# Summing four query-key chunks of the last block by accumulating DMAs instead of pair adds on GpSimd

## The chip, the cores and the metric

One core of one Trainium2 chip runs the whole kernel. The metric is the device time of one execution in microseconds (us). A single core has no die to compare with, so a run is called fast when it lies within 1.5% of the fastest run of the same kernel. Ratios are the mean time of one kernel's fast runs over the mean of the other's fast runs of the same rounds, so they are not quite the ratio of the medians quoted beside them.

Engines: PE is TensorE's matmuls, PEld its weight loads, DVE is VectorE, ACT is ScalarE, POOL is GpSimd, SP is SyncE, which issues most DMAs. "L816" is line 816 of the kernel. The change adds 25 lines in the middle, so lines below it move: L816 becomes L841, L1052 becomes L1077, and so on.

## The reference, cut to what matters

```python
xn = _layernorm(x)                                   # 2048 positions x 640
# A: local attention, 32 heads of 20, window of 8 keys at distance 0, 2, ..., 14
logits = einsum("bhsd,bhswd->bhsw", q, kg) * scale   # kg: keys gathered at the 8 offsets
attn   = softmax(where(mask, logits, -1e9))
o      = einsum("bhsw,bhswd->bhsd", attn, vg)
# B: gated branch
h      = (xn @ w_gate) * (xn @ w_up)                 # 640 -> 1536
return x + o.reshape(...) @ wo + h @ w_down
```

The 2048 positions are handled as four blocks `j` of 512. The 640 columns of q and k are five chunks `c` of 128 partitions. With 20 columns per head, a head is spread so that each chunk holds four elements of every head.

## The kernel before: the parts that matter

A query-key logit is made in two steps. VectorE multiplies q by a shifted k, elementwise. TensorE then sums the products over partitions and chunks with a 0/1 matrix `G`. For most blocks that is five chunks, so five accumulating terms per head sum. In the last block (`WIDE`) the first four chunks take q straight from PSUM, give FP32 products in half-size pieces (`PRD32`), and GpSimd adds two chunks at a time. Three terms remain: chunks 0+1, chunks 2+3, and chunk 4. There are two key halves `r`, so six terms, and four matmuls for each.

```python
def pair_add(j, s, n, q0, f, parts):                 # last block only
    a, b = PRD32[f[0]], PRD32[f[1]]
    o = s[:, q0:q0 + 2, :]
    def go():
        op("pool", lambda e: e.tensor_tensor(o, a[:], b[:], ALU.add), ..., occ=2.36, lock=True)
        free.extend(f)
        parts.append(q0)
    yield Task("pool", go, ..., prio=5, lock=True)

def logits(j, slots):                                # the head sums on TensorE (L816)
    ...
    yield Task("pe", go, r=[e[1][:] for e in slots], prio=9.5, banks=2, slack=0.5)
    bump("lg")
```

The program of each engine is fixed while the kernel is built. A list scheduler in the kernel's own code takes tasks in order of an assumed time. For that it uses a duration per operation (`occ`) and, for a DMA, a byte count (`nbytes`) and an added delay (`extra`). On the chip a late input holds up everything behind it in the list: in the traces here TensorE stands still for up to 13.77 us at one such input.

Three gates hang on the last head-sum block:

```python
def vx_loads():                  # values for the weighted sums; they reuse q's memory
    yield num(NJ, "lg")          # all four head-sum blocks have been placed
    ...
def weighted():                  # PV = attention weight x value on VectorE (L962),
    ...                          # pair adds on GpSimd (L967), select-sums on TensorE (L1008)
def gu(j):                       # gate and up projections, 12 pairs per block, PE filler
    ...
    if j == 1 and m == 6:
        yield num(NJ, "lg")      # pair 19 and later reuse a product buffer
```

The weighted stage has 20 units (block x chunk). A select-sum takes three units at a time. The down projection `dn(j)` needs all units of its block and is also what lets the gate/up pairs of the fourth block start.

## Time and profile before

| | before |
|---|---|
| two runs | 271.29 and 348.41 us (median 309.85) |
| profiled run | 271.47 us, span 269.7 us |
| 23 further runs, on three later occasions | 271.06 to 272.17 us |

The first and fourth parts of the page: busy time, share of the span and instruction count by engine, then the chain of work that ended last.

```profile
PE 264.3 (98%) x1791; PEld 152.7 (57%) x1791; DVE 231.9 (86%) x294; ACT 98.4 (36%) x175; POOL 115.2 (43%) x65
...
PE 96%; DVE 2%; DMA 1%; issue 0%; DVEq 0%
```

TensorE is the limit almost everywhere. The windows of before show the second limit. Columns: the stretch, its length, then busy us and instruction count of PE, PEld, DVE, ACT and POOL, granted TensorE clock, DMA share, GB/s.

```profile
80.00:108.00 28.00, 28.00 (x145) 12.78 (x145) 25.25 (x29) 7.66 (x13) 18.41 (x8) 1.00 0.61 141
108.00:121.00 13.00, 13.00 (x74) 5.75 (x63) 12.79 (x14) 6.78 (x10) 3.27 (x1) 1.00 0.55 146
...
160.00:180.00 20.00, 20.00 (x150) 13.36 (x148) 18.54 (x17) 2.45 (x5) 15.45 (x7) 1.00 0.52 137
```

Third busy number: VectorE is busy 38.0 of the 41 us from 80 to 121 us. It has almost nothing to give away, although TensorE is the engine that never stops.

The timeline of TensorE before, at two places: the last head sums (L816), and the select-sum of units 3 to 5 (L1008) with the first down projection (L1110) after it. Columns: start, duration, engine, line, operation, output<-inputs, shapes, count; brackets would show idle time and who ended it.

```profile
107.20 1.48 PE L816 MATMUL PS<-PRD,G 128*32 128x512 bf16 x24
108.61 1.25 PE L1052 MATMUL PS<-XNT,WG 128*128 128x512 bf16 x5
...
162.10 0.83 PE L1008 MATMUL PS<-SV,SEL 128*32 128x512 bf16 x12
162.87 1.80 PE L1110 MATMUL PS<-WD,HT 128*128 128x320 bf16 x12
```

No wait of PE shows at either place.

### The profile page before, as it was taken

The numbers are of one execution on the slowest core, as the hardware profiler recorded it, in microseconds if no ns is written. First come the engines' busy times: TensorE is split into PE (matmuls) and PEld (weight loads), VectorE is DVE, ScalarE is ACT, GpSimd is POOL, SyncE is SP. The second block draws the span as 40 slices with busy tenths as digits, with TensorE's granted clock in tenths as the row PEclk, the third lists the DMA queues.
The fourth block names the chain that finished last, engine by engine and source line by source line (L and its number), as shares of the span: only waits on it lengthen the run. The fifth ranks groups of instructions, "written<-read, shape, count | busy, mean of one in ns | idle before, by whom it ended". The sixth has DMA issues, their size and how long they took to land.

```text
span 269.7 us, 4474 instructions
## 1 busy us (share of the span) xinstructions
PE 264.3 (98%) x1791; PEld 152.7 (57%) x1791; DVE 231.9 (86%) x294; ACT 98.4 (36%) x175; POOL 115.2 (43%) x65
## 2 busy tenths in 40 slices
PE   7999999999999999999999999999999999999995
PEld 4896965544444444443444446764447767654775
DVE  4778899999999997999999999989999998984221
ACT  2469998557632123632324422015240120033000
POOL 1000000000018763042776676957868679755000
DMA  7966479322325934901295333555333655220101
GB/s 209 366 198 86 99 124 381 158 97 97 104 44 163 216 66 130 282 5 30 52 256 125 86 79 79 155 153 130 79 80 106 175 135 148 66 81 2 49 27 50
DMA packets 39717, 33.49 MB, mean 124 GB/s; under 512 B 15376, under 2 KB 38416, under 8 KB 39696
## 3 DMA queue, kind: packets, MB, share of 16 engines
q1 hardware_dynamic: 39408, 33.15, 45.8%
q8 instruction: 14, 0.23, 0.4%
q10 hardware_dynamic: 288, 0.05, 0.1%
q14 instruction: 7, 0.06, 0.1%
HBM read 25.08 MB, written 5.26 MB: 112 GB/s over the span
## 4 chain that ended last, share of the span: by engine, by line
PE 96%; DVE 2%; DMA 1%; issue 0%; DVEq 0%
PE PS L1052 38%; PE PS L1110 28%; PE PS L610 24%; PE PS L816 3%; PE PS L1008 2%; DMA XST<-in_A_x_dram 1%; PE PS L569 1%; DVE STATS L525 0%; DVE XNT L578 0%; DVE HT L1061 0%; DVE XNS L543 0%; DVE FOUT L1121 0%; DVE MV L528 0%; DVE SD L536 0%; DVEq L319 0%
## 5 line engine op out<-in xcount | busy, mean ns | idle before, releaser
L967 POOL TENSOR_TENSOR SV<-PV 128x1024 bf16<-128x1024 f32 x40 | 94.7, 2378 | 48.4 <-DVE PV L962 48.3
L962 DVE TENSOR_TENSOR PV<-VX,PS 128x1024 f32<-128x1024 bf16 (+1 forms) x56 | 92.7, 1670 | 0.0
L610 PE MATMUL PS<-XNT,WQKV 128*128 128x512 bf16 (+2 forms) x480 | 67.0, 299 | 0.8 <-DVE XNT L578 0.8
L1052 PE MATMUL PS<-XNT,WU 128*128 128x512 bf16 x240 | 59.7, 379 | 0.5 <-DVE HT L1061 0.5
L1052 PE MATMUL PS<-XNT,WG 128*128 128x512 bf16 x240 | 59.7, 379 | 0.0
L610 PEld LDWEIGHTS PS<-XNT,WQKV 128*128 128x128 bf16 x480 | 43.4, 114 | 23.4 <-DVE XNT L578 1.5
L1110 PE MATMUL PS<-WD,HT 128*128 128x320 bf16 (+1 forms) x300 | 43.3, 294 | 0.0
L615 ACT ACTIVATE HT<-PS 128x512 bf16<-128x512 f32 x36 | 21.5, 597 | 53.2 <-PE PS L1052 53.1
L1052 PEld LDWEIGHTS PS<-XNT,WU 128*128 128x128 bf16 x240 | 23.3, 98 | 29.3 <-DVE HT L1061 1.0
L1052 PEld LDWEIGHTS PS<-XNT,WG 128*128 128x128 bf16 x240 | 23.2, 98 | 28.7 <-issue 0.8
L738 DVE TENSOR_TENSOR PRD<-QT,KT 128x2048 bf16<-128x2048 bf16 x32 | 36.8, 1218 | 0.0
L1110 PEld LDWEIGHTS PS<-WD,HT 128*128 128x128 bf16 x300 | 28.5, 98 | 11.6 <-issue 1.3
L794 POOL TENSOR_TENSOR PRD<-PRF,PRF 128x1024 bf16<-128x1024 f32 x8 | 18.8, 2357 | 35.5 <-DVE PRF L780 35.5
L1121 DVE TENSOR_TENSOR FOUT<-PS,XR 128x320 bf16<-128x320 f32 (+1 forms) x33 | 15.8, 478 | 18.3 <-PE PS L1110 18.2
L1061 DVE TENSOR_TENSOR HT<-HT,PS 128x512 bf16<-128x512 bf16 x36 | 24.1, 682 | 6.8 <-PE PS L1052 5.6
L1110 PE MATMUL PS<-WO,OT 128*128 128x320 bf16 (+1 forms) x165 | 27.1, 295 | 0.0
L835 POOL MEMSET LOG<- 32x6 bf16 (+6 forms) x7 | 0.4, 95 | 46.6 <-ACT LOG L827 46.6
L1017 ACT ACTIVATE OT<-PS 128x512 bf16<-128x512 f32 x20 | 10.5, 597 | 25.1 <-PE PS L1008 25.1
L1110 PEld LDWEIGHTS PS<-WO,OT 128*128 128x128 bf16 x165 | 15.9, 98 | 5.9
L780 DVE TENSOR_TENSOR PRF<-PS,KT 128x1024 f32<-128x1024 f32 x16 | 19.0, 1218 | 0.3 <-PE PS L816 0.2
L525 DVE BATCH_NORM_STATS2 STATS<-XST 128x6 f32<-128x320 bf16 x32 | 14.7, 469 | 2.0 <-DMA XST<-in_A_x_dram 2.0
L947 ACT ACTIVATE PS<-ATX 128x512 f32<-128x512 bf16 x8 | 4.8, 598 | 27.4 <-DVE PV L962 27.4
(47 smaller groups left out, 162.3 us busy)
## 6 DMA issues: line engine op xcount, KB each, us to landing
VX<-v_scratch SPq DMA_DIRECT2D x80, 130.0 KB, 2.9
XST<-in_A_x_dram SPq DMA_DIRECT2D x16, 160.0 KB, 6.3
v_scratch<-VST SPq DMA_DIRECT2D x4, 640.0 KB, 4.4
XR<-in_A_x_dram SPq DMA_DIRECT2D x16, 160.0 KB, 3.3
out_dram<-FOUT SPq DMA_DIRECT2D x15, 160.0 KB, 2.0
WG<-in_B_w_gate_dram SPq DMA_DIRECT2D x1, 1920.0 KB, 7.6
WU<-in_B_w_up_dram SPq DMA_DIRECT2D x1, 1920.0 KB, 11.8
WD<-in_B_w_down_dram SPq DMA_DIRECT2D x1, 1920.0 KB, 8.6
```

The costliest lines, as they stand in the source:

```text
L525: op("dve", lambda e: e.bn_stats(o, a), r=[a], w=[("st", t, i)], name=f"bn{t}_{i}", occ=0.49)
L610: op("pe", (lambda o, l, x, c, first: lambda e: e.matmul(o, l, x, start=first, stop=(c == NCH - 1)))(o, l, x, c, first), r=[l, x], w=[o], ...
L615: X = op("act", (lambda o, i: lambda e: e.activation(o, i, ACT.Copy))(o, i), r=[i], w=[o], name=name, occ=0.12 + n * 0.9e-3)
L738: op("dve", lambda e: e.tensor_tensor(s[:], qb, kv, ALU.mult), r=[q, rk], w=[s[:]], name=f"prod{j}_{r}_{c}", occ=1.15, lock=True)
L780: X = op("dve", lambda e: e.tensor_tensor(o[:], qb, kv, ALU.mult), r=[q, rk], w=[o[:]], name=f"prow{j}_{r}_{c}_{q0}", occ=1.17)
L794: op("pool", lambda e: e.tensor_tensor(o, a[:], b[:], ALU.add), r=[a[:], b[:]], w=[o], name=f"padd{j}_{n}_{q0}", occ=2.36, lock=True)
L962: op("dve", lambda e: e.tensor_tensor(p, vw, a, ALU.mult), r=[vv] + rk, w=[p], name=f"pv{u}_{x}_{r0}", occ=0.09 + 1.1 * nr)
L967: X = op("pool", lambda e: e.tensor_tensor(o, p[:, :, 0, :], p[:, :, 1, :], ALU.add), r=[p[:]], w=[o], name=f"pva{u}_{x}", occ=2.36, lock= ...
L1052: op("pe", (lambda l, x, c: lambda e: e.matmul(PS[:, b, :], l, x, start=(c == 0), stop=(c == NCH - 1)))(l, x, c), r=[l, x], w=[PS[:, b, :] ...
L1061: X = op("dve", lambda e: e.tensor_tensor(h, h, PS[:, hold[1], :], ALU.mult), r=[h, PS[:, hold[1], :]], w=[h], name=f"h{m}_{j}", occ=0.65)
L1110: op("pe", (lambda l, x, i: lambda e: e.matmul(dst, l, x, start=(i == 0), stop=(i == n - 1)))(l, x, i), r=[l, x], w=[PS[:, b, :]], name=f" ...
L1121: X = op("dve", lambda e: e.tensor_tensor(o, PS[:, b, 0:wid], xr, ALU.add), r=[PS[:, b, :], xr], w=[o], name=f"fin{t}_{nb}", occ=0.15 + wi ...
```

## The change

The intent: add up all four chunks before TensorE sees them, with DMAs that add what they carry to what lies at the destination (`accum_op`), so that GpSimd does less and only two terms per head sum remain. Eight matmuls fall away. Core of the diff (cut):

```diff
+    def accum(name, a, b):
+        o, i = PRD32[a][:], PRD32[b][:]
+        op("pool", lambda e: e.dma_start(o, i, accum_op=ALU.add), r=[o, i], w=[o], dma=True, name=name, nbytes=1048576,
+           occ=1.0, extra=1.0)
+
+    def gather(name, a, b):                      # chunk pair: a += b; b's buffer is free when it lands
         ...
+    def close(tag, r, q0, acc, f, n, parts):     # chunks 2+3, then onto chunks 0+1
+        yield from gather(f"qacc{tag}_1", *f)
         ...
+        if r:                                    # one more accumulate, and a DMA that casts to BF16
+            yield Task("pool", lambda: accum(f"qacc{tag}_2", acc, f[0]), ...)
+            yield Task("pool", cast, r=[a[:]], w=[o], prio=5)
+        else:                                    # or an add on GpSimd
+            yield Task("pool", add, r=[a[:], b[:]], w=[o], prio=5, lock=True)
-    def pair_add(j, s, n, q0, f, parts):
         ...
-            op("pool", lambda e: e.tensor_tensor(o, a[:], b[:], ALU.add), ..., occ=2.36, lock=True)
```

In all there are ten accumulating DMAs of 512 KB, two casting DMAs of 256 KB and two GpSimd adds, in place of eight GpSimd adds. And because the scheduler assumes long DMAs, the order of everything after them changes. This is TensorE's list from the third head-sum block on (matmul counts; gu = gate/up, 10 per pair; lg = head sums; I = select-sum; dn = down projection):

```
before  lg40 gu35 qkv10 gu80  lg24 gu150 I12 gu90 I12 dn136 I12 gu80 I12 dn136 I12 dn35 I12 dn5 gu40 I8 dn153
changed lg40 gu35 qkv10 gu140 lg16 gu160 I12 gu20 I12 dn119 I12 dn17 gu75 I12 gu5 dn136 I12 dn119 ...
```

More of the change, by code (lines that the diff above doesn't have):

```diff
@@ L755, in wide @@
     def wide(j, slots):
+        sums, parts, dest = {}, {1: [], 0: []}, {}
         for c0 in (0, 2):
@@ L761, in wide @@
                 K.spawn(q_bank(j, c, hold[c]))
-            last = None
             for r in (1, 0):
-                yield lambda: len(free) > 0
-                n = slot()
-                s = PRD[n]
-                parts = []
+                if c0:
+                    yield lambda: len(free) > 0
+                    dest[r] = slot()
                 for q0 in (0, 2):
@@ L785, in wide, with add, cast @@
                         yield Task("dve", go, r=[q, rk], w=[o[:]], prio=20 + j)
-                    K.spawn(pair_add(j, s, n, q0, f, parts))
-                slots.append((n, s, r, parts))
-    def pair_add(j, s, n, q0, f, parts):
-        a, b = PRD32[f[0]], PRD32[f[1]]
-        o = s[:, q0:q0 + 2, :]
-        def go():
-            op("pool", lambda e: e.tensor_tensor(o, a[:], b[:], ALU.add), r=[a[:], b[:]], w=[o], name=f"padd{j}_{n}_{q0}",
-               occ=2.36, lock=True)
-            free.extend(f)
-            parts.append(q0)
-        yield Task("pool", go, r=[a[:], b[:]], w=[o], prio=5, lock=True)
+                    tag = f"{j}_{r}_{q0}"
+                    if c0 == 0:
+                        sums[r, q0] = f[0]
+                        K.spawn(gather(f"qacc{tag}", f[0], f[1]))
+                    else:
+                        K.spawn(close(tag, r, q0, sums[r, q0], f, dest[r], parts[r]))
+        for r in (1, 0):
+            slots.append((dest[r], PRD[dest[r]], r, parts[r]))
+    def accum(name, a, b):
[3 more added lines that the diff above has]
+    def gather(name, a, b):
+        def go():
+            accum(name, a, b)
+            free.append(b)
+        yield Task("pool", go, r=[PRD32[a][:], PRD32[b][:]], w=[PRD32[a][:]], prio=5)
+    def close(tag, r, q0, acc, f, n, parts):
+        yield from gather(f"qacc{tag}_1", *f)
+        o, a, b = PRD[n][:, q0:q0 + 2, :], PRD32[acc], PRD32[f[0]]
+        def add():
+            op("pool", lambda e: e.tensor_tensor(o, a[:], b[:], ALU.add), r=[a[:], b[:]], w=[o], name=f"padd{tag}",
+               occ=2.36, lock=True)
+        def cast():
+            op("pool", lambda e: e.dma_start(o, a[:]), r=[a[:]], w=[o], dma=True, name=f"qcast{tag}", nbytes=786432,
+               occ=1.0, extra=1.0)
+        if r:
+            yield Task("pool", lambda: accum(f"qacc{tag}_2", acc, f[0]), r=[a[:], b[:]], w=[a[:]], prio=5)
+            yield Task("pool", cast, r=[a[:]], w=[o], prio=5)
+        else:
+            yield Task("pool", add, r=[a[:], b[:]], w=[o], prio=5, lock=True)
+        free.extend((acc, f[0]))
+        parts.append(q0)
     def logits(j, slots):
```

## The prediction

> **What bounds the kernel now.** TensorE. The page has PE busy 264.3 of 269.7 us (98%), and the chain that ended last is 96% PE. VectorE is nearly a second limit (231.9 us): the windows leave it only about 8 us of idle between 121 and 247 us. GpSimd (43%) mostly waits for VectorE.
>
> **Removed.** Two of six terms per head-sum block: 8 of 24 L816 matmuls. The 24 took 107.20 to 108.61 us in the timeline, so 8 are worth about 0.45 us, on the critical path. Six of eight GpSimd pair adds (2.36 us each, 14 us) go too, off the path and worth nothing directly.
>
> **Added.** Ten accumulating DMAs of 512 KB FP32 and two casting DMAs, on GpSimd's queue. This trace has none. A plain 640 KB store landed in 4.4 us. The Trainium skill ("DMA: Bandwidth & Descriptors", the SWDGE anatomy section) gives about 2.0 us + bytes/436 GB/s; counting source and destination reads (1 MB) my estimate is 4.5-6 us each, perhaps more, as the DMA engines are already 61% busy from 80 to 108 us. VectorE products now wait for them in program order, because product buffers come free only when a DMA lands.
>
> **Moved; this decides it.** Comparing instruction orders, the last head-sum block slides behind six more gate/up pairs (18 instead of 12 since the first), 6 x 2.16 us = 13 us: from 107.2 to about 120 us. The weighted-value stage (PV products, adds) sits behind it in VectorE's order, so it starts at about 121 instead of 108 us. VectorE can fill that gap only with the six extra HT products (0.6 us each, 3.6 us), so it loses about 9 us that it cannot spare.
>
> PE runs out of other work: in the new order all 36 gate/up pairs of the first three blocks are done (about 161 us), and then it needs the select-sum of units 3-5 before any down projection. Adding VectorE durations from the trace (P2 2.2, single PV 1.15, HT 0.6, softmax about 11 us) from 121 us, unit 5's products end at about 169.5 us and its two GpSimd adds at about 173 us. Before, this point came at 162.1 us without a wait. So PE idles 11-12 us there, and both engines run on shifted. After such a pause the clock gate may halve TensorE's speed for about 3.4 us ("TensorE: Matmul & The Clock Gate", table of the two states), up to 1.7 us more; this trace has no such pause.
>
> **Sum.** -0.45 + 11.5 + about 1.3 = +12.3 us. Against the fast run of 271.3 us: 284 us, range 277 to 298. Chances: faster 0.02, same 0.12, slower 0.86. (The 348 us run is left out as slow.)
>
> **What the profile would show.** The L816 group (renumbered) x136 instead of x144; head sums of the last block at about 120 us; VectorE idle 9 us more between 80 and 121 us; a TensorE gap of about 11 us near 161-174 us released by GpSimd's adds; DMA time from issue to landing 4.5-6 us for the accumulates; the tail after the last select-sum unchanged.
>
> **What would make it wrong.** Accumulates much slower than 6 us: VectorE then waits on buffers, HT products and PSUM banks come late, PE waits already at 85-120 us, and the total goes toward 295 or more. Or PE has work in the gap that I read as blocked, then the time stays within 2%.

## The result, and the profile after

| | before | changed |
|---|---|---|
| runs of the first comparison | 271.29 us (and one of 348.41) | 285.26 and 288.84 us, median 287.05 |
| ratio of fast runs | | 1.057, 95% interval 1.048 to 1.067 |
| repeated later | 271.46, 271.47 us | 286.47, 286.45 us; ratio 1.057 and 1.055 |
| span of the profiled run | 269.7 us | 283.5 us |

The change costs 15 us by the medians of the later calls, 13.8 us in the profiled run of the first. Busy times, the clock in 40 slices (tenths of full speed, 9 is 90% or more), and the chain that ended last, from the page after:

```profile
PE 266.6 (94%) x1783; PEld 153.1 (54%) x1783; DVE 232.7 (82%) x294; ACT 98.3 (35%) x175; POOL 109.9 (39%) x71
...
PEclk9999999999999999999999985999999999999999
...
PE 81%; DMA 10%; DVE 4%; POOL 2%; issue 1%; DVEq 0%
```

PE has eight instructions less and yet a longer span. DMA has come onto the chain with 10%, which invites the reading "the DMAs are too slow". The experiments will show that this reading is half of the truth.

The same windows, after (a DMA share above 1 means that the times of packets overlap):

```profile
80.00:108.00 28.00, 28.00 (x131) 12.88 (x130) 22.83 (x26) 7.16 (x12) 8.07 (x10) 1.00 1.05 218
108.00:121.00 13.00, 11.99 (x56) 5.21 (x54) 7.01 (x8) 3.58 (x6) 5.81 (x4) 1.00 0.99 208
...
160.00:180.00 20.00, 9.70 (x47) 4.24 (x45) 17.84 (x16) 3.51 (x6) 16.65 (x8) 0.74 0.43 107
```

From 80 to 121 us VectorE is now idle 11.2 us (41 - 22.83 - 7.01) where it was idle 3.0. In that stretch TensorE loses one us. The weighted stage starts late: its first products on VectorE, before and after, stand here.

```profile
107.98 2.35 DVE L962 TENSOR_TENSOR PV<-VX,PS 128x1024 f32<-128x1024 bf16 x2
...
123.33 1.22 DVE L987 TENSOR_TENSOR PV<-VX,PS 128x1024 f32<-128x1024 bf16 x1 [1.41 <-ACT PS L972]
```

That is 15.3 us. TensorE pays later: from 160 to 180 us it works 9.7 of 20 us, at a granted clock of 0.74. The timeline of TensorE after shows where:

```profile
121.54 1.05 PE L841 MATMUL PS<-PRD,G 128*32 128x512 bf16 x16 [1.55 <-DMA PRD<-PRF]
...
162.34 0.77 PE L1033 MATMUL PS<-SV,SEL 128*32 128x512 bf16 x4
167.95 0.43 PE L1033 MATMUL PS<-SV,SEL 128*32 128x512 bf16 x2 [4.84 <-POOL SV L992]
170.25 0.61 PE L1033 MATMUL PS<-SV,SEL 128*32 128x512 bf16 x2 [1.87 <-POOL SV L992]
172.75 0.61 PE L1033 MATMUL PS<-SV,SEL 128*32 128x512 bf16 x2 [1.90 <-POOL SV L992]
175.06 0.61 PE L1033 MATMUL PS<-SV,SEL 128*32 128x512 bf16 x2 [1.69 <-POOL SV L992]
175.60 3.16 PE L1135 MATMUL PS<-WD,HT 128*128 128x320 bf16 x12
```

The select-sum of units 3 to 5 starts at about the same time as before (162.34 against 162.10 us), but its inputs drip in one by one, each released by a GpSimd add of the weighted stage, and the down projection starts at 175.60 instead of 162.87 us. The first twelve down matmuls then take 3.16 us instead of 1.80. The account of the two profiled runs: +0.2 us up to the select-sum, +12.5 us in it (13.26 against 0.77 us), +1.1 us from there to the end (107.9 against 106.8 us). Sum 13.8 us, the difference of the spans. The first repeat of the changed kernel (span 284.8 us, further down) gives +1.0, +12.5 and +1.6 us, together 15.1.

### The profile page after: what moved, and what is told of

Read it like the earlier page. It is cut to its first block, busy times and chain, and to the rows that moved or that the text cites. A ratio compares the mean times of both kernels' runs of the same rounds, so it can differ in the third digit from the quotient of the medians.

```text
span 283.5 us, 4466 instructions
## 1 busy us (share of the span) xinstructions
PE 266.6 (94%) x1783; PEld 153.1 (54%) x1783; DVE 232.7 (82%) x294; ACT 98.3 (35%) x175; POOL 109.9 (39%) x71
## 4 chain that ended last, share of the span: by engine, by line
PE 81%; DMA 10%; DVE 4%; POOL 2%; issue 1%; DVEq 0%
PE PS L1135 27%; PE PS L1077 26%; PE PS L610 23%; DMA PRF<-PRF 7%; PE PS L841 3%; POOL SV L992 2%; DMA PRD<-PRF 2%; PE PS L1033 2%; DVE PRF L779 2%; DVE PV L987 1%; DMA XST<-in_A_x_dram 1%; PE PS L569 1%; DVE STATS L525 0%; DVE XNT L578 0%; DVE HT L1086 0%
## 5 line engine op out<-in xcount | busy, mean ns | idle before, releaser
L992 POOL TENSOR_TENSOR SV<-PV 128x1024 bf16<-128x1024 f32 x40 | 93.6, 2355 | 45.8 <-DVE PV L987 45.6
L1135 PE MATMUL PS<-WD,HT 128*128 128x320 bf16 (+1 forms) x300 | 44.6, 300 | 0.0
L738 DVE TENSOR_TENSOR PRD<-QT,KT 128x2048 bf16<-128x2048 bf16 x32 | 38.5, 1268 | 0.0
L1135 PEld LDWEIGHTS PS<-WD,HT 128*128 128x128 bf16 x300 | 29.1, 100 | 12.4 <-issue 0.4
L796 POOL DMA_DIRECT2D PRF<-PRF x10 | 8.8, 875 | 50.1 <-DVE PRF L779 47.1
L1033 PE MATMUL PS<-SV,SEL 128*32 128x512 bf16 x80 | 7.8, 401 | 10.3 <-POOL SV L992 10.3
```

The costliest lines, as they stand in the source:

```text
L738: op("dve", lambda e: e.tensor_tensor(s[:], qb, kv, ALU.mult), r=[q, rk], w=[s[:]], name=f"prod{j}_{r}_{c}", occ=1.15, lock=True)
L992: X = op("pool", lambda e: e.tensor_tensor(o, p[:, :, 0, :], p[:, :, 1, :], ALU.add), r=[p[:]], w=[o], name=f"pva{u}_{x}", occ=2.36, lock= ...
L1033: op("pe", (lambda o, p, dq: lambda e: e.matmul(o, SEL[:], p, start=True, stop=True, tile_position=(0, 32 * dq)))(o, p, dq), r=[SEL[:], p] ...
L1135: op("pe", (lambda l, x, i: lambda e: e.matmul(dst, l, x, start=(i == 0), stop=(i == n - 1)))(l, x, i), r=[l, x], w=[PS[:, b, :]], name=f" ...
```

## The experiments

Theory ORDER: the last head-sum block now stands behind 18 gate/up pairs instead of 12. The weighted stage stands behind it, so VectorE starves before it, and TensorE starves when its filler is used up at 162 us. Rival DMA: the accumulating DMAs themselves, their time and the load they put on the DMA engines, make the loss.

### The late place without any DMA

The kernel before, with one number changed.

```diff
-        yield Task("pe", go, r=[e[1][:] for e in slots], prio=9.5, banks=2, slack=0.5)
+        yield Task("pe", go, r=[e[1][:] for e in slots], prio=9.5, banks=2, slack=13.5 if j == NJ - 1 else 0.5)
```

> The kernel before, no DMA and no new sum: only the scheduler is told that the last head-sum block is ready 13 us later, so that it slides behind 18 gate/up pairs as in the changed kernel. Theory ORDER (the late block starves VectorE, and TensorE then waits for units 3-5): TensorE gap of 9-12 us near 160-175 us, total 280 to 284 us, ratio to before about 1.04. Rival DMA (the accumulating DMAs' time and load make the loss): nothing is left to cause it, 271 to 273 us, ratio within 1.01.

Measured: 285.90 us against 271.63 us, ratio 1.052 (1.050 to 1.054), result correct. The waits of PE in this run (who waited <- for whom: us in total, times, longest):

```profile
PE PS L1008 <- POOL SV L967: 9.8, 5, 3.5
```

The same wait as in the changed kernel, in a kernel with no new DMA and the old sums. The late place alone is enough for 14.3 us of loss, nearly all of the 15.0 us of the changed kernel. This kernel makes all 24 head-sum matmuls, too.

### The changed order with DMAs that move almost nothing

Here the list of every engine is that of the changed kernel. Only the regions of the DMAs shrink, so the result is wrong (relative error 0.36).

```diff
-        op("pool", lambda e: e.dma_start(o, i, accum_op=ALU.add), ...
+        op("pool", lambda e: e.dma_start(o[:, 0, 0:16], i[:, 0, 0:16], accum_op=ALU.add), ...
-            op("pool", lambda e: e.dma_start(o, a[:]), ...
+            op("pool", lambda e: e.dma_start(o[:, 0, 0:16], a[:, 0, 0:16]), ...
```

> The changed kernel in its exact instruction order, but each accumulating or casting DMA moves only 16 elements per partition (the result is wrong on purpose). Theory ORDER: DMAs land in about 2-3 us, the 1.5 us wait of TensorE at the head sums vanishes, but the gap near 160-175 us stays at 9-11 us: total 282 to 284 us, ratio about 1.045. Rival DMA: with the DMA time gone the loss goes, 271 to 273 us.

Measured: 285.99 us, ratio 1.053. The accumulates now land in 2.5 us (median; 9.2 us in the first trace of the changed kernel), and next to nothing is won: 0.5 us against the changed kernel (286.47 us), less than the runs of either kernel differ among themselves. The waits of PE:

```profile
PE PS L1033 <- POOL SV L992: 10.1, 4, 4.8
...
PE PS L841 <- DVE PRD L738: 1.2, 1, 1.2
```

The second line corrects a detail. The 1.5 us wait at the head sums is put down to a DMA in the changed kernel. With the DMA gone it is 1.2 us and waits for VectorE's last product, which stands behind the HT product of pair 18. It belongs to the order too.

### Half the delay: the same sums by GpSimd adds

Four chunks are still summed in FP32 and two terms remain, but by twelve GpSimd adds.

```diff
-        op("pool", lambda e: e.dma_start(o, i, accum_op=ALU.add), ..., dma=True, nbytes=1048576, occ=1.0, extra=1.0)
+        op("pool", lambda e: e.tensor_tensor(o, o, i, ALU.add), ..., occ=2.36, lock=True)
-        if r: (accumulate and cast by DMA)
-        else:
+        if True:
             yield Task("pool", add, ...)
```

> The changed sums (four chunks in FP32, two terms per head sum), made by twelve GpSimd adds of 2.36 us instead of DMAs. The scheduler then puts the block behind about 15.5 pairs, 7 us later than before instead of 13. Theory ORDER: half of the gap, 3-7 us, total 274 to 279 us. Rival DMA: no accumulating DMA, so 270.5 to 273 us.

Measured: 280.40 us, ratio 1.031, correct. It lies above my range, but with the theory: the head sums start at 114.86 us, 7.7 us later than before, PE waits 6.3 us for the select-sum's inputs, and the loss is 8.8 us. I had expected to lose only half the delay. The loss is a little more than the delay.

### Letting the weighted stage start before the head sums

An attempt at a remedy. The last chunk's products go first, the weighted stage is gated on the last product rather than on the head sums, and units 0 and 1 may pass.

```diff
     def vx_loads():
-        yield num(NJ, "lg")
+        yield have("prod", NJ - 1)
 ...
+        if u == 2:
+            yield num(NJ, "lg")
-            o, p = SV[u % NS][...]                # the first two units must not use buffers
+            o, p = SV[(u + 3) % NS][...]          # that the head sums still read
```

(The other uses of `SV` follow, and the products of chunk 4 are moved in front of the wide part.)

> The changed kernel with its DMAs, but the last chunk's products go first, and the first two units of the weighted-value stage may go before the last head-sum block. The block stays at about 120 us. Theory ORDER: VectorE has work while the DMAs run, the select-sum of units 3-5 is ready near 163 us, and the gap shrinks to under 3 us: total 271 to 276 us. Rival DMA: the DMAs are as before, and so is the loss: 282 to 287 us.

Measured: 289.53 us, ratio 1.066, correct. The expectation failed. The gap at the select-sum is gone, but a new one stands at the head sums:

```profile
120.29 0.40 PE L842 MATMUL PS<-PRD,G 128*32 128x512 bf16 x4
121.95 0.61 PE L842 MATMUL PS<-PRD,G 128*32 128x512 bf16 x8 [1.26 <-DMA PRD<-PRF]
136.34 0.62 PE L842 MATMUL PS<-PRD,G 128*32 128x512 bf16 x4 [13.77 <-POOL PRD L812]
```

The timeline of the other engines tells why. VectorE's last two wide products came only at 121.07 us, behind HT products that keep TensorE's pace and after waits for product buffers. Their accumulate was issued at 123.72 us and landed 4.5 us later. The closing add then stood in GpSimd's list behind three adds of the weighted stage (126.90 to 133.98 us). My reordering moved the wait instead of removing it.

### The early place with the real DMAs

The changed kernel, with the scheduler told that the DMAs are short.

```diff
-        ... nbytes=1048576, occ=1.0, extra=1.0)      # accumulate
+        ... nbytes=131072, occ=1.0, extra=0.0)
-        ... nbytes=786432, occ=1.0, extra=1.0)       # cast
+        ... nbytes=131072, occ=1.0, extra=0.0)
```

> The changed kernel, only the scheduler is told that its DMAs are short, so that the last head-sum block is placed behind 13 gate/up pairs instead of 18; the DMAs still move everything. Theory BOTH (placing the block early helps only if the sums are ready): TensorE waits 8-11 us at the head sums near 109-120 us, the gap near 163 us shrinks, total 281 to 286 us. Rival ORDER ALONE (the DMAs would be fast enough if the block stood early): 272 to 275 us.

Measured: 294.35 us, ratio 1.085, correct. Worse than the late place, and by more than either theory said. The waits of PE:

```profile
PE PS L1077 <- DVE PRF L779: 9.2, 2, 8.6
PE PS L841 <- POOL PRD L811: 7.3, 1, 7.3
PE PS L1033 <- POOL SV L992: 1.7, 1, 1.7
```

The gap at the select-sum has shrunk to 1.7 us, as the place is early. But VectorE waits for a product buffer that a DMA still reads (its longest idle time in the timeline is 10.22 us, ended by an accumulate), HT products queue behind it in VectorE's list, and the gate/up matmuls, whose PSUM banks those products empty, wait 8.6 us. Then TensorE waits 7.3 us at the head sums.

### Early place and tiny DMAs together

Both edits, wrong result.

> Both at once: the early order of e5_optimist, and DMAs of 16 elements per partition (wrong result on purpose). Theory BOTH: block early and sums ready, so neither wait is left: 271 to 274 us, ratio within 1.01. If four chunks summed in FP32 cost by themselves (buffers, waits of VectorE), it stays over 278 us.

Measured: 274.31 us, ratio 1.011 (1.009 to 1.012). PE waits 1.6 us at the head sums and 1.7 us at the select-sum. Less the 0.45 us for eight matmuls, that is the 2.9 us that are left. So the new sums cost little by themselves. Together with the runs above this makes a square:

| median us (before: 271.5) | DMAs move 512 KB | DMAs move 16 elements per partition |
|---|---|---|
| block behind 18 pairs | 286.5 | 286.0 |
| block behind 13 pairs | 294.4 | 274.3 |

Taking the DMA time away alone wins 0.5 us. Moving the block forward alone loses 8. Only both together win 12. No place between 13 and 18 pairs was tried with the real DMAs, so whether one of them beats 286.5 us stays open.

### The clock after the pause

The changed kernel with 50 matmuls on a zero tile, never read, in the pause.

```diff
+            if 5 in us:
+                for _ in range(50):
+                    op("pe", lambda e: e.matmul(PS[:, bs[0], :], ZERO[:, 0:128], ZERO[:], start=True, stop=True), ...)
```

> The changed kernel with 50 idle matmuls (10.8 us, never read) put where TensorE waits for units 3-5. Theory CLOCK (the pause halves the TensorE clock for a while afterwards): the first down projection takes 1.8 us as elsewhere instead of 3.2 us, total 1.0 to 1.8 us under the changed kernel of the same call. Rival (the slow first group is a wait for data, not the clock): no change, within 0.4 us.

Measured: 284.10 us against 286.47 us for the changed kernel. The first down matmuls in this run:

```profile
175.48 1.80 PE L1139 MATMUL PS<-WD,HT 128*128 128x320 bf16 x12
177.12 0.84 PE L1139 MATMUL PS<-WO,OT 128*128 128x320 bf16 x5
177.80 1.79 PE L1139 MATMUL PS<-WD,HT 128*128 128x320 bf16 x12
```

and in the repeat of the changed kernel:

```profile
176.37 3.38 PE L1135 MATMUL PS<-WD,HT 128*128 128x320 bf16 x12
179.54 1.18 PE L1135 MATMUL PS<-WO,OT 128*128 128x320 bf16 x5
180.56 1.66 PE L1135 MATMUL PS<-WD,HT 128*128 128x320 bf16 x11
```

The first 17 matmuls take 4.19 us in the repeat (176.37 to 180.56) and 2.32 us with the filler (175.48 to 177.80). So the pause costs 1.9 us of clock here, and the granted clock of the run rises from 0.976 to 1.000 with the filler. By the same count it costs 1.4 us in the first trace of the changed kernel and 2.3 us in its last repeat. The spans of the two runs differ by 2.7 us; the other 0.8 us is a different wait at the head sums, 1.2 us in this trace and 2.0 in the other, which moves from run to run. The Trainium skill ("TensorE: Matmul & The Clock Gate", Part 1) says that an idle TensorE falls to half its clock after an idle window of about 3.4 us and needs about as long to recover. The traces agree on the half clock: the granted clock is 0.50, and the twelve matmuls took 1.8 to 1.9 times as long. On the times they agree only roughly: the clock fell 2.7 us after the last matmul before the pause in the repeat and 5.1 us after it in the first trace, and came back 3.8 and 2.8 us into the down projection.

The reference:

> The changed kernel once more, as reference for this call: 285 to 288 us, ratio 1.05 to 1.06.

Measured: 286.47 us, ratio 1.057.

### The load on the DMA engines

The changed kernel with the first 16 VX loads made to wait for an HT product of about 111 us. The lists of TensorE and VectorE stay the same.

```diff
-                    dma(dst, src, r=rk, w=[dst], ...)
+                    dma(dst, src, r=rk + ([ht(1, 1)] if u < NVX else []), w=[dst], ...)
```

> The changed kernel, same instruction order on TensorE and VectorE; only the first 16 VX loads wait for an HT product of about 111 us, so that they no longer share the DMA engines with the accumulates. Theory LOAD (the accumulates take 9.5 us instead of 5 because of the VX loads beside them): their median falls to 5-7 us, TensorE's wait at the head sums of 1-2 us goes, the total falls by 1 to 2 us against the changed kernel of the same call, the gap at 163 us stays. Rival (the accumulates load the engines by themselves): median stays at 8-10 us, total unchanged.

The time from issue to landing of the ten accumulates, in this run and then in the changed kernel:

```profile
DMA to landing us min/median/max: 4.6/6.5/8.6
```

```profile
DMA to landing us min/median/max: 5.0/9.3/10.9
```

The load is real: without the VX loads beside them the accumulates land in two thirds of the time. But the kernel takes 286.67 us against 286.45 us of the reference, ratios 1.054 and 1.055. The 1-2 us that I expected are not there. PE waits 1.2 us at the head sums all the same, for VectorE's last product. In this order the DMAs' time is hidden.

> The changed kernel as reference for this call: 285 to 288 us.

Measured: 286.45 us.

### A candidate and its control

The GpSimd adds of the third experiment with the reordering of the fourth:

> Candidate: the four-chunk sums by GpSimd adds as in e3_pool_adds, with the last chunk's products first and two weighted units ahead of the last head-sum block as in e4_ahead. Theory ORDER: VectorE is fed while the adds run, no gap over 3 us: 270.5 to 275 us. At best 0.45 us under before. Rival (GpSimd becomes the limit with 4 more adds): over 277 us.

Measured: 290.10 us, and the result is wrong (relative error 0.59), which was not intended. With GpSimd busier, its adds of the weighted stage are placed later than VectorE's next products, which go into the same few buffers. The scheduler has no guard for that, so the add of unit 0 reads a product of unit 1: in the trace unit 1's first product starts at 114.83 us, the first add only at 117.19. The time is far from the 270.5 to 275 us of the theory, and TensorE's longest wait is 7.9 us, at a select-sum. As the result is wrong by accident, I draw nothing more from it.

The kernel before with that reordering alone:

> Control: the kernel before with that same reordering alone, sums unchanged. TensorE is 98% busy already, so nothing to win: 270.5 to 273 us.

Measured: 272.93 us, ratio 1.005 (1.004 to 1.007), correct. As expected nothing is won, and 1.5 us are lost; one wait of 1.8 us for an HT product shows in its trace. No version beat the kernel before. The most that the idea could win is the 0.45 us of eight matmuls.

### The places and the losses in one table

"Last head sums" is the start of the last group of head-sum matmuls in the trace (a group is an unbroken stretch, here of 4 to 24 matmuls, so the column is exact only to a us or so); "later" is against 107.20 us of before; the loss is the difference of the medians. The run with the filler matmuls and the wrong candidate are left out.

| kernel | last head sums, us | later | loss, us |
|---|---|---|---|
| before, reordered (control) | 111.01 | 3.8 | 1.5 |
| early place, tiny DMAs | 111.99 | 4.8 | 2.9 |
| twelve GpSimd adds | 114.86 | 7.7 | 8.8 |
| before, placed late | 120.03 | 12.8 | 14.3 |
| changed, VX loads late | 121.96 | 14.8 | 15.2 |
| changed (repeat) | 122.30 | 15.1 | 15.0 |
| late place, tiny DMAs | 122.34 | 15.1 | 14.4 |
| early place, real DMAs | 130.21 | 23.0 | 22.9 |
| weighted stage ahead | 136.34 | 29.1 | 17.9 |

In the rows from 7.7 to 15.1 us the loss follows the delay nearly one to one, whether a DMA, an add or a bare number in the scheduler made it; below that a part of the delay is free. The row of 23.0 us fits in number only: there most of the loss is TensorE's own waiting before and at the head sums (9.2 and 7.3 us). The last row breaks the rule. There VectorE had done part of the weighted stage before the head sums, and 11 of the 29 us were not lost; TensorE's waits at the head sums (13.8 and 1.3 us) are most of what was. That the early part of the weighted stage saved the 11 us fits, but no run shows it alone.

## Why the prediction was right or wrong, point by point

- **The number: wrong as a comparison with the printed median.** 284 us is inside the range and close to the 285 to 288 us measured. But the printed time of before is a median of 309.85 us, and beside it 284 reads as 8% faster, while the text says 86% for slower. The step that failed there is the comparison under "Sum": 284 stands "against the fast run of 271.3 us", and the prediction did not restate it for the printed median. As a time of the kernel before, 271.3 us was right: 23 later runs took 271.06 to 272.17 us. Against 271.3 us the forecast was +4.7%; the measured ratio is +5.7%.
- **The sum itself: one term mis-sized, and it moved the rest.** Predicted -0.45 + 11.5 + about 1.3 = +12.3 us. Measured +0.2, +12.5 and +1.1 in the first profiled run, and +1.0, +12.5 and +1.6 in the repeat. The step that failed is the first term with "6 x 2.16 us = 13 us" under "Moved". It lets the last head sums start, and the weighted stage after them, when the last filler pair is done, at about 120 us. In its place the runs show a further wait of 1.5 to 2.0 us there, most of it for VectorE's last product (see the removed matmuls below). The sum had no term for it.
- **The block slides and VectorE starves: right in kind, the slide too short.** Predicted about 120 us for the head sums, measured 121.54 and in the repeat 122.30. Predicted about 121 us for the weighted stage, measured 123.33, which is 15.3 us later than before and not 13. Predicted 9 us more VectorE idle from 80 to 121 us, measured 8.2. Moving the block late in the old kernel gave nearly all of the loss by itself.
- **The gap: right in place and cause, slightly small.** Predicted 11-12 us near 161-174 us, released by GpSimd's adds. Measured 12.5 us more than before, from 162.3 to 175.6 us. The last add came at 175.0 us instead of the predicted 173, about as much later as the weighted stage had started late.
- **The clock: right in kind, its upper bound too low.** Predicted about 1.3 us, with an estimate of up to 1.7. Measured 1.4 us in the first profiled run, 1.9 us by the experiment with filler matmuls and 2.3 us in the last repeat.
- **The removed matmuls: right and small.** x136 instead of x144. Their 0.45 us can't be seen alone: up to the select-sum the changed kernel is 0.2 us later, not earlier, as the head sums wait 1.5 us (2.0 in the repeat). That wait was missing in the sum. I let the block start at 120.2 us and forgot that its last product stands behind the HT product of pair 18. With the DMAs' time taken away 1.2 us of the wait remain, and it is that product that TensorE waits for.
- **The DMA's time: mis-sized.** Predicted 4.5-6 us each, "perhaps more"; measured 9.2 us median, 4.9 to 10.9. The first, issued with only 32 KB ATX loads beside it, took 4.9 us, as estimated. The load beside them was much of the error: the DMA engines went from a share of 0.61 to 1.05 in that window, and without the VX loads the median was 6.5 us. I had made "much slower than 6 us" the main risk for a total of 295 us or more; at 9.2 us the total was 285 to 289. The longer time cost next to nothing in this order, because the scheduler had reserved room for it: with tiny DMAs in the same order only 0.5 us were won. With the block placed early it would have been the largest term, as the run of 294 us shows.

So the cause has two halves that don't add. The DMAs are slow, and at the one earlier place that was tried this cost more than standing late; standing late is what the changed kernel pays. Of the two, removing one alone did not help: the loss stayed or grew.

## What to carry to other kernels

Ask of a replacement not only what it costs but how late its result comes, and which stage is queued behind that result on an engine with no slack: here 15 us of delay cost 15 us although TensorE had filler work for another 40 us. When DMA stands on the chain of waits, test whether shortening it alone helps before believing it, since an order fixed in advance can have paid for it already. And state a forecast against the same base in the text and in the number.

## What the Trainium skill lacked or had wrong

- "DMA: Bandwidth & Descriptors" says that accumulation is possible only from GpSimd's queue, but gives no time for it. Its fit for a DMA from that queue ("Anatomy of one DMA — SWDGE (gpsimd) path": about 2.0 us plus bytes over 436 GB/s) gives 3.2 us for 512 KB, or 4.4 us if the destination read is counted as well. Measured: 4.9 us for the first accumulate, 6.5 us median with the VX loads out of the way, 9.2 us with them. The fixed part agrees: 16 elements per partition landed in 2.2 us (median, early place).
- The same page's list of where the fixed time goes calls descriptor generation "small, variable", with no figure; its latency table gives about 1 us to the first byte from this queue. In these traces issuing one accumulate held GpSimd for 0.86 us (median of ten), the same when it moved only 16 elements per partition. That is a third of the 2.36 us of a GpSimd add.
- No page says how much an accumulating stream slows the DMAs beside it. Here issuing the 16 VX loads took SP 18.1 us with the accumulates beside them, instead of 8.3 us before; with tiny accumulates in the same order it took 8.2 us.
- "TensorE: Matmul & The Clock Gate" was borne out: half speed after a pause whose longest idle stretch was 4.8 us, and 1.4 to 2.3 us lost.
